# Retention and PReLU MLP on one core: scores and carried sums as one product of 128 rows, q and k turned by VectorE for all pairs from the second batch on

## The chip, the core and the metric

One core of a Trainium2 chip runs the whole program. The metric is the device time of one execution in microseconds (us). TensorE multiplies, VectorE, ScalarE and GpSimd (POOL) work elementwise, and SyncE (SP) issues nearly all transfers.

## What is computed

For 8 batches and 8 heads, q, k and v are 576 x 64 each. The attention is a retention with a decay of each head, without softmax; its output is one token-by-512 matrix, which goes through a two-layer MLP with a PReLU of 2048 features:

```python
scores = scale * np.matmul(q, k.transpose(0, 1, 3, 2))
gamma = 1.0 - 2.0 ** (-5.0 - np.arange(H, dtype=np.float32))
Dmat = np.where(rel >= 0, gamma[:, None, None] ** rel[None, :, :], 0.0)
attn_out = np.matmul(scores * Dmat[None, :, :, :], v)
x = attn_out.transpose(0, 2, 1, 3).reshape(B * S, H * D)     # 4608 x 512
h = x @ w_in
g = np.maximum(h, 0.0) + alpha * np.minimum(h, 0.0)
return g @ w_out
```

All data is fp32.

## The kernel before

**Attention.** A sequence is cut into NJ = 9 chunks of C = 64 positions, and two heads make a pair: 4 pairs for each batch, 32 in all. In a chunk the masked scores act on v directly; what earlier chunks bring comes through carried sums of k transposed times v (a 64 x 64 matrix for each chunk and head), which multiply q. The decay is put in by scaling q and v by powers of gamma, by a factor in the masked scores (L577) and in the running sums. The first batch (pairs 0 to 3) is worked in parts of its own (`part_...`, L627 to L772), which the change leaves as they are. Every other pair passes through these steps:

- *turning*: q and k have to stand with the 64 features on the partitions. For the pairs of batch 1 (4 to 7; `n < NEARLY`) they are loaded in natural order and TensorE turns them (`turn`, L542): five products with an identity (L552) for each of k and q, and two copies by ScalarE (L555). For the pairs from batch 2 on they are loaded in strips (`load_sq`, L84) of 32 features, so that VectorE's turn of 32 x 32 squares (L539) does it; k is then loaded a second time in natural order for the sums. GpSimd scales q (L534, or L515) and v (L515).
- `scores` (L564): 64 x 64 products for both heads, 20 for a pair (chunk 9 is done twice to fill the tile, L573), into two PSUM tiles, one for each head; VectorE scales and masks them into `at` (L577).
- `states` (L582): 16 products of 64 x 64 (L588), then ScalarE's copy (L593) and VectorE's running sums (L594, L597, L599) into `su`.
- `values` (L606): 18 products of v with the masked scores (L612), and on top of them in the same PSUM tiles 32 products of 64 rows and 32 columns with the sums as weights and q as the moving operand (L619). ScalarE puts the result into the token blocks `xb` (`put_x`, L503 and L505).

**MLP.** 18 blocks of 256 tokens. The first two are worked plainly (`plain_unit` L397, `plain_out` L376), while the weights arrive in 32 pieces that ScalarE, VectorE and GpSimd round (`piece_in`, `piece_out`). The other 16 use a product scheme with 7 products instead of 8 (`mlp_unit`): for each of 8 units of a block 14 products with 128 columns moving (L441), elementwise steps on ScalarE and VectorE (L447 to L463), and 7 products with 256 columns moving (L361), which are issued one unit later. At the end of a block VectorE combines the PSUM tiles (L347, L348), and two transfers store the block.

**What orders the work.** Up to L889 the order is the program's own. The 12 units of the plain stage (L874) have 21 gaps, and `gap` (L861) puts one step of the list `steps` into each: k, q, u (states), s, v for each of the four pairs of batch 1, with the scaling ahead of k. The loads of pair n + 2 are issued behind the values of pair n. From L894 on, the loop over pairs interleaves the attention of one batch with the MLP units of the blocks that are ready (`pop_units`): scores, units, states, units, the turning of the next pair, values, units; here a scheduler places the instructions. All PSUM tiles of the attention share one tag with two buffers (`ps_tile`, L520). `kT` and `at` have one buffer, `qT` and `su` two, and the loaded tiles two.

Of the kernel before, what the change touches and what calls it, by code (L numbers as in the profile page):

```python
# [18 lines left out]
def kernel(  # L19
# [49 lines left out]


    NEARLY = 2 * NPAIR

    def load_nat(t, src, b, c):
        hs, s0 = slice(2 * c, 2 * c + 2), (NM - 1) * P
        for h2 in range(2):
            nc.sync.dma_start(t[:, 0:NM - 1, h2],
                              src[b, 2 * c + h2, 0:s0].rearrange("(m p) d -> p m d", p=P))
        nc.sync.dma_start(t[0:C, NM - 1], src[b, hs, s0:S].rearrange("h p d -> p h d"))  # L80
# [9 lines left out]

    def load_pair(n):
        b, c = pairs[n]
        kn, vn, qx = [nat.tile([P, NM, 2, D], FP32, tag=f"nat_{x}", name=f"{x}n_{n}")
                      for x in "kvq"]
        if n < NEARLY:
            kx = kn
            load_nat(kn, k, b, c)
            load_nat(qx, q, b, c)
        else:
            kx = nat.tile([P, NB, 32], FP32, tag="sq_k", name=f"kx_{n}")  # L100
            qx = qx.rearrange("p m h d -> p (m h d)")[:, 0:S].rearrange(
                "p (n r) -> p n r", r=32)
            load_sq(kx, k, b, c)
            load_sq(qx, q, b, c)
            load_nat(kn, k, b, c)
        load_nat(vn, v, b, c)
        return kn, kx, qx, vn
# [55 lines left out]
    make_identity(nc, ident)  # L163

# [46 lines left out]
    tabx = const.tile([P, NPAIR, 2], FP32, name="tabx")  # L211
    for h2 in range(2):
        hd = slice(h2 * D, (h2 + 1) * D)
        nc.vector.tensor_copy(gch[hd, 0], th[hd, 2, h2:H:2])
        nc.vector.tensor_scalar(tabx[hd, :, 0], pf[hd, 0, h2:H:2], float(D) ** -0.5, None,
                                ALU.mult)
        nc.vector.scalar_tensor_tensor(out=tabx[hd, :, 1], in0=dif[hd, 5, h2:H:2], scalar=1.0,
                                       in1=tabx[hd, :, 0], op0=ALU.add, op1=ALU.mult)
# [272 lines left out]
    def put_x(b, c, par, pv):  # L491

        w = TB // C
        at = b * NJ
        m, nm = 0, NM - par
        while m < nm:
            kb, o = divmod(at + 2 * m + par, w)
            if kb not in xb:
                xb[kb] = ring.tile([P, NCC, TB], FP32, tag=f"x{kb % NRING}", name=f"xb_{kb}")
            n = min(nm - m, (w - o + 1) // 2)  # L500
            to = xb[kb][:, c].rearrange("p (j w) -> p j w", w=C)[:, o:o + 2 * n - 1:2]
            for h2 in range(2) if par else ():
                nc.scalar.copy(to[half(h2)], pv[half(1 - h2), m:m + n])  # L503
            if not par:
                nc.scalar.copy(to, pv[:, m:m + n])  # L505
            m += n
# [3 lines left out]


    def scale(t, x, c):
        for rows, m in ((P, slice(0, NM - 1)), (C, slice(NM - 1, NM))):
            n = m.stop - m.start
            nc.gpsimd.tensor_tensor(  # L515
                out=t[0:rows, m], in0=t[0:rows, m],
                in1=th[0:rows, x, None, 2 * c:2 * c + 2, None].to_broadcast([rows, n, 2, D]),
                op=ALU.mult)
# [4 lines left out]
    def scale_pair(n):  # L523
        c = pairs[n][1]
        scale(loaded[n][2], 0, c)
        scale(loaded[n][3], 1, c)

    def transposes(n):
        c = pairs[n][1]
        kn, kx, qx, vn = loaded[n]  # L530
        kT = attn.tile([P, S], FP32, tag="kT", name=f"kT_{n}")
        qT = attn.tile([P, S], FP32, tag="qT", bufs=2, name=f"qT_{n}")
# [4 lines left out]
        scale(vn, 1, c)  # L537
        for src, dst in ((kx, kT), (qx, qT)):
            nc.vector.transpose(dst, src.rearrange("p n r -> p (n r)"))  # L539
        return kT, qT  # L540

    def turn(n, i):  # L542

        src = loaded[n][i]
        dst = attn.tile([P, S], FP32, tag="qT" if i else "kT", bufs=2 if i else 1,
                        name=f"T{i}_{n}")
        for m0, m1 in ((0, 3), (3, NM)):
            w = min(m1 * P, S) - m0 * P
            pt = ps_tile([P, 3 * P], f"pt{i + m0}_{n}")
            for m in range(m0, m1):  # L550
                rows = min(P, S - m * P)
                nc.tensor.transpose(pt[:, (m - m0) * P:(m - m0) * P + rows],  # L552
                                    src[0:rows, m].rearrange("p h d -> p (h d)"),
                                    ident[0:rows, 0:rows])
            nc.scalar.copy(dst[:, m0 * P:m0 * P + w], pt[:, 0:w])  # L555
        return dst

    def half(x):
        return slice(x * C, (x + 1) * C)
# [4 lines left out]
    def scores(n, kT, qT):  # L564
        c = pairs[n][1]
        at = attn.tile([P, 2 * NM * C], FP32, tag="at", name=f"at_{n}").rearrange(
            "p (h m s) -> h p m s", h=2, s=C)
        ps = [ps_tile([P, NM, C], f"ps{h2}_{n}") for h2 in range(2)]
        for m in range(NM):
            for p2 in range(2):  # L570
                j = min(2 * m + p2, NJ - 1)
                for h2 in range(2):
                    nc.tensor.matmul(ps[h2][half(p2), m], kT[half(h2), chunk(j)],  # L573
                                     qT[half(h2), chunk(j)], start=True, stop=True)
        for h2 in range(2):
            h = 2 * c + h2
            nc.vector.scalar_tensor_tensor(  # L577
                out=at[h2], in0=ps[h2], scalar=th[:, 3, h:h + 1],
                in1=mask[:, None, :].to_broadcast([P, NM, C]), op0=ALU.mult, op1=ALU.mult)
        return at  # L580

    def states(n, kn, vn):  # L582
        c = pairs[n][1]
        ps = [ps_tile([P, NM - 1, D], f"pu{p2}_{n}") for p2 in range(2)]
        for m in range(NM - 1):
            for p2 in range(2):
                for h2 in range(2):
                    nc.tensor.matmul(ps[p2][half(h2), m], kn[half(p2), m, h2],  # L588
                                     vn[half(p2), m, h2], start=(m == 0), stop=(m == NM - 2),
                                     skip_group_check=True)  # L590
        su = attn.tile([P, NJ - 1, D], FP32, tag="su", bufs=2, name=f"su_{n}")
        g1, g2 = gch[:, 0, c:c + 1], gch[:, 1, c:c + 1]
        nc.scalar.copy(su[:, 0::2], ps[0])  # L593
        nc.vector.scalar_tensor_tensor(out=su[:, 1::2], in0=su[:, 0::2], scalar=g1, in1=ps[1],  # L594
                                       op0=ALU.mult, op1=ALU.add)
# [5 lines left out]
        return su  # L601

    def values(n, vn, qT, at, su):  # L606
        b, c = pairs[n]
        pv = [ps_tile([P, NM, C], f"pv{p2}_{n}") for p2 in range(2)]
        for m in range(NM):
            for p2 in range(2 if 2 * m + 1 < NJ else 1):  # L610
                for h2 in range(2):
                    nc.tensor.matmul(pv[p2][half(h2 ^ p2), m], vn[half(p2), m, h2],  # L612
                                     at[h2][half(p2), m], start=(m == 0), stop=False,
                                     skip_group_check=True)
        for j in range(1, NJ):
            for h2 in range(2):
                for e in range(0, D, 32):
                    to = (h2 ^ (j % 2)) * D + e
                    nc.tensor.matmul(pv[j % 2][to:to + 32, j // 2],  # L619
                                     su[half(h2), j - 1, e:e + 32], qT[half(h2), chunk(j)],  # L620
                                     start=False, stop=(j >= NJ - 2), skip_group_check=True)
        for p2 in range(2):
            put_x(b, c, p2, pv[p2])
# [215 lines left out]
    kq, ats, sus = {}, {}, {}  # L839

    def step(what, n):
        kn, _, _, vn = loaded[n]
        if what == "scale":
            scale_pair(n)
        elif what in "kq":
            kq[n] = kq.get(n, ()) + (turn(n, 0 if what == "k" else 2),)
        elif what == "s":
            ats[n] = scores(n, *kq[n])
        elif what == "u":
            sus[n] = states(n, kn, vn)  # L850
        elif what == "v":
            values(n, vn, kq[n][1], ats[n], sus[n])
            del loaded[n]
            if n + 2 <= NEARLY:
                loaded[n + 2] = load_pair(n + 2)

    steps = [(x, n) for n in range(NPAIR, NEARLY) for x in "kqusv"]
    scale_pair(NPAIR)
    scaled = [NPAIR + 1]

    def gap():  # L861

        for x, n in steps[0:3]:
            if x == "k" and n == scaled[0] and n in loaded:
                scaled[0] += 1
                step("scale", n)
        if steps:
            step(*steps.pop(0))
# [77 lines left out]
```

## Time and profile before

| | |
|---|---|
| median of 3 runs | 1047.41 us (1045.88 to 1048.51) |
| the profiled execution | 1043.84 us, its span 1042.1 us |
| granted TensorE clock | 0.997 |
| attention products of pairs 4 to 31, busy: values L612, L619 | 22.3 + 24.0 us |
| scores L573, states L588 | 22.7 + 19.4 us |
| turning on TensorE, L552 | 7.0 us |
| MLP products L441 and L361 | 491.2 and 407.8 us |
| squares on VectorE, L539 | 37.1 us for 48 |

Each row of the page's table of groups gives a line of the kernel, the engine and operation, the tiles, the shape and the number of instructions, then the busy time of the group, the mean time of one in ns, and the idle time of the engine just ahead of them with what ended it. Products overlap in the array: 1008 records of L612 with a mean of 223 ns are 22.3 us of busy time. So the cost of a block of small products is read from the timeline, from its first start to the start of what follows it. A product of fp32 operands leaves two records. PE is TensorE's row for products, PEld the one for loading weights.

### The profile page before, as it was taken

The numbers are of one execution on the slowest core, as the hardware profiler recorded it, in microseconds if no ns is written. First come the engines' busy times: TensorE is split into PE (matmuls) and PEld (weight loads), VectorE is DVE, ScalarE is ACT, GpSimd is POOL, SyncE is SP. The second block draws the span as 40 slices with busy tenths as digits, with TensorE's granted clock in tenths as the row PEclk, the third lists the DMA queues.
The fourth block names the chain that finished last, engine by engine and source line by source line (L and its number), as shares of the span: only waits on it lengthen the run. The fifth ranks groups of instructions, "written<-read, shape, count | busy, mean of one in ns | idle before, by whom it ended". The sixth has DMA issues, their size and how long they took to land.

```text
span 1042.1 us, 27067 instructions
## 1 busy us (share of the span) xinstructions
PE 1024.3 (98%) x11329; PEld 902.0 (87%) x11329; DVE 748.2 (72%) x1951; ACT 170.8 (16%) x533; POOL 214.8 (21%) x253
## 2 busy tenths in 40 slices
PE   5999999999999999999999999999999999999998
PEld 4766667999999999999999999999999999999997
DVE  7766755776786778776768777867777776766675
ACT  4545532111111110110110011111111111000000
POOL 4566675411301020200011111301030001010000
PEclk8999999999999999999999999999999999999999
DMA  9855605233232221121212232222222100000000
GB/s 244 252 153 139 163 20 122 41 68 64 48 67 45 59 47 44 35 56 24 56 36 50 42 68 46 57 47 53 62 40 52 24 22 2 21 1 22 1 21 21
DMA packets 216073, 63.36 MB, mean 61 GB/s; under 512 B 201088, under 2 KB 209296, under 8 KB 215952
## 3 DMA queue, kind: packets, MB, share of 16 engines
q1 hardware_dynamic: 213840, 61.11, 25.3%
q8 instruction: 89, 1.46, 0.6%
q10 hardware_dynamic: 2112, 0.53, 0.3%
q14 instruction: 32, 0.26, 0.1%
HBM read 52.17 MB, written 9.44 MB: 59 GB/s over the span
## 4 chain that ended last, share of the span: by engine, by line
PE 97%; DMA 1%; issue 1%; POOL 0%; DVE 0%; ACT 0%; SPq 0%; DVEq 0%; POOLq 0%
PE ph L441 40%; PE po L361 37%; PE ph L397 6%; PE po L376 5%; PE pv L619 2%; PE ps L573 2%; PE pv L612 2%; PE pu L588 2%; DMA w_out<-in_k_dram 1%; PE pt L552 0%; PE pt L653 0%; PE pv L726 0%; PE ps L672 0%; PE pv L715 0%; POOL w_out L304 0%
## 5 line engine op out<-in xcount | busy, mean ns | idle before, releaser
L361 PE MATMUL po<-w_out,g 128*128 128x256 f32 x1792 | 407.8, 379 | 0.0
L361 PEld LDWEIGHTS po<-w_out,g 128*128 128x128 f32 x1792 | 330.8, 190 | 39.7
L452 DVE TENSOR_TENSOR g<-ph,g 128x256 f32<-128x256 f32 (+1 forms) x512 | 187.4, 387 | 176.6 <-PE ph L441 95.7
L441 PE MATMUL ph<-xb,w_in 128*128 128x128 f32 x2048 | 277.6, 278 | 0.0
L441 PEld LDWEIGHTS ph<-xb,w_in 128*128 128x128 f32 x2048 | 253.2, 192 | 9.2 <-issue 0.7
L441 PE MATMUL ph<-xt,w_in 128*128 128x128 f32 x1536 | 213.6, 275 | 0.0
L441 PEld LDWEIGHTS ph<-xt,w_in 128*128 128x128 f32 x1536 | 192.2, 192 | 0.1
L463 DVE TENSOR_TENSOR g<-g 128x128 f32<-128x128 f32 x512 | 143.0, 320 | 7.8
L447 ACT COPY g<-ph 128x128 f32<-128x128 f32 x128 | 34.0, 265 | 462.2 <-PE ph L441 457.3
L515 POOL TENSOR_TENSOR vn<-vn,th 128x512 f32<-128x512 f32 (+1 forms) x56 | 39.7, 729 | 336.0 <-DMA vn<-in_v_dram 315.2
L455 DVE TENSOR_SCALAR g<-g,alpha 128x256 f32<-128x256 f32 x256 | 92.1, 402 | 4.5
L457 DVE SCALAR_TENSOR_TENSOR g<-g 128x512 f32<-128x512 f32 x128 | 91.8, 717 | 3.8
L397 PE MATMUL ph<-xb,w_in 128*128 128x256 f32 x256 | 61.1, 394 | 1.1 <-ACT xb L733 1.1
L427 POOL TENSOR_TENSOR xt<-xb,xt 128x256 f32<-128x256 f32 x32 | 25.2, 788 | 172.3 <-ACT xb L505 163.3
L376 PE MATMUL po<-w_out,g 128*128 128x512 f32 x128 | 59.0, 604 | 0.1
L397 PEld LDWEIGHTS ph<-xb,w_in 128*128 128x128 f32 x256 | 49.2, 196 | 10.0 <-issue 2.4
L503 ACT COPY xb<-pv 64x64 f32<-64x64 f32 (+1 forms) x144 | 33.9, 236 | 145.7 <-PE pv L619 143.9
L376 PEld LDWEIGHTS po<-w_out,g 128*128 128x128 f32 x128 | 23.1, 190 | 24.3 <-issue 22.5
L539 DVE STREAM_TRANSPOSE qT<-qn 128x576 f32<-128x576 f32 x24 | 18.7, 778 | 28.9 <-PE pv L619 23.1
L413 DVE SCALAR_TENSOR_TENSOR g<-g,nalpha,ph 128x256 f32<-128x256 f32 x32 | 13.9, 477 | 31.6 <-ACT ph L403 31.6
L534 POOL TENSOR_TENSOR qn<-qn,tabx 128x576 f32<-128x576 f32 x24 | 28.1, 1171 | 28.7 <-DMA qn<-in_q_dram 22.8
L427 POOL TENSOR_TENSOR xt<-xb 128x256 f32<-128x256 f32 x16 | 11.5, 722 | 107.3 <-PE ph L441 107.3
(127 smaller groups left out, 665.0 us busy)
## 6 DMA issues: line engine op xcount, KB each, us to landing
out_dram<-osb SPq DMA_DIRECT2D x36, 256.0 KB, 2.2
kn<-in_k_dram SPq DMA_DIRECT2D x56, 128.0 KB, 2.9
vn<-in_v_dram SPq DMA_DIRECT2D x56, 128.0 KB, 2.8
kx<-in_k_dram SPq DMA_DIRECT2D x96, 72.0 KB, 2.5
qn<-in_q_dram SPq DMA_DIRECT2D x96, 72.0 KB, 2.6
raw<-in_moe_w_in_dram SPq DMA_DIRECT2D x24, 256.0 KB, 4.2
raw<-in_moe_w_out_dram SPq DMA_DIRECT2D x10, 512.0 KB, 4.5
w_in<-in_moe_w_out_dram SPq DMA_DIRECT2D x6, 512.0 KB, 4.8
```

The costliest lines, as they stand in the source:

```text
L361: nc.tensor.matmul(acc[kb][n // 2][:, n % 2, :], g[:, x, :], w_out[i][:, y, :], start=(i == 0 and n % 2 == 0), stop=(i == NU - 1 and (n % ...
L376: nc.tensor.matmul(acc[kb][m], g[:, 2 * x + m], w_out[i][:, 2 * x:2 * x + 2].rearrange("p x f -> p (x f)"), start=(i == 0 and x == 0), sto ...
L397: nc.tensor.matmul(ph[:, x], w_in[i // UST][:, cc // 2 * 2 + x, i % UST, cc % 2], xb[kb][:, cc], start=(cc == 0 and x == 0), stop=(cc == N ...
L427: nc.gpsimd.tensor_tensor(out=o, in0=x0, in1=x1, op=ALU.subtract)
L441: nc.tensor.matmul(ph[m][:, o], w_in[i // UST][:, l, i % UST, cc], r[:, cc], start=(n in (0, 3) and cc == 0), stop=(n in (2, 6) and cc == ...
L447: nc.scalar.copy(g[:, 7], ph[0][:, 2])
L452: nc.vector.tensor_tensor(out=o, in0=x0, in1=x1, op=ALU.add)
L455: nc.vector.tensor_scalar(g[:, 4 + 2 * m:6 + 2 * m], g[:, 2 * m:2 * m + 2], 0.0, alpha[:, fc:fc + 1], ALU.min, ALU.mult)
L457: nc.vector.scalar_tensor_tensor(out=g[:, 0:4].rearrange("p x t -> p (x t)"), in0=g[:, 0:4].rearrange("p x t -> p (x t)"), scalar=0.0, in1 ...
L463: ins = nc.vector.tensor_tensor(out=g[:, o, :], in0=g[:, x0, :], in1=g[:, x1, :], op=op)
L503: nc.scalar.copy(to[half(h2)], pv[half(1 - h2), m:m + n])
L515: nc.gpsimd.tensor_tensor(out=t[0:rows, m], in0=t[0:rows, m], in1=th[0:rows, x, None, 2 * c:2 * c + 2, None].to_broadcast([rows, n, 2, D]) ...
```

## The change

All pairs from pair 4 on now take one path.

- Loading: every pair has q and k in strips (`kx`, `qx`), and k (`kn`) and v (`vn`) for each head with the chunk's 64 positions on the partitions; head 0 lies on the upper half of them, head 1 on the lower. 12 loads for a pair. In `vn` the other half of the partitions of each head is kept for the sums; its chunk 0 is filled with zeros by ScalarE.
- Scaling: GpSimd scales q alone, ScalarE scales v (`tabv`). This is a step of its own ("p"), before the values of the pair ahead.
- Scores: 18 products. Both heads of a chunk go to one PSUM tile, on different halves of its partitions, and the tiles alternate by chunk. ScalarE copies the turned q into one half of the partitions of `mt`; VectorE writes the masked scores into the other half, in four instructions.
- States: again 16 products; the first step of the sums is two instructions of 64 partitions. The sums take the buffer of `kT`, and ScalarE copies them into `vn` behind v.
- Values: one product of 128 rows (64 of v, 64 of the sums) and 64 columns for each chunk and head, 18 for a pair; ScalarE's copies into `xb` are three for a pair.
- Order: in the gaps of the plain stage the steps are t, s, u, p, v of each pair, with the turning "t" of the next pair right behind v. Pair 8 is turned there too, and one MLP unit now comes ahead of its scores.

```diff
-    NEARLY = 2 * NPAIR
+    def load_head(t, src, b, h):
+        nc.sync.dma_start(t, src[b, h].rearrange("(j t) d -> t j d", t=C))
+
     def load_pair(n):
         b, c = pairs[n]
...
+        load_sq(kx, k, b, c)
+        load_sq(qx, q, b, c)
+        for t, src in ((vn, v), (kn, k)):
+            for h2 in range(2):
+                load_head(t[half(1 - h2), h2] if t is vn else t[half(1 - h2)], src, b, 2 * c + h2)
+        for h2 in range(2):
+
+            nc.scalar.copy(vn[half(h2), h2, 0], zero[half(h2)])
...
     def scale_pair(n):
         c = pairs[n][1]
-        scale(loaded[n][2], 0, c)
-        scale(loaded[n][3], 1, c)
...
+        for h2 in range(2):
+            x = half(1 - h2)
+            nc.scalar.activation(vn[x, h2], vn[x, h2], ACTF.Copy, scale=tabv[x, c:c + 1])
...
-    def turn(n, i):
...
+    def pair_scores(n, kT, qT):
...
+        ps = [ps_tile([P, NM, C], f"ps{p2}_{n}") for p2 in range(2)]
+        for j in range(NJ):
+            for h2 in range(2):
+                x = (1 - h2, h2)[j % 2]
+                nc.tensor.matmul(ps[j % 2][half(x), j // 2], kT[half(h2), chunk(j)],
+                                 qT[half(h2), chunk(j)], start=True, stop=True)
         for h2 in range(2):
...
+            nc.scalar.copy(mt[half(h2), h2].rearrange("p j s -> p (j s)"), qT[half(h2)])
+        for p2 in range(2):
+            for h2 in range(2):
+                h, to, x = 2 * c + h2, half(1 - h2), (1 - h2, h2)[p2]
+                nm = NM - p2
+                nc.vector.scalar_tensor_tensor(
+                    out=mt[to, h2, p2::2], in0=ps[p2][half(x), 0:nm], scalar=th[to, 3, h:h + 1],
+                    in1=mask[to, None, :].to_broadcast([C, nm, C]), op0=ALU.mult, op1=ALU.mult)
+        return mt
...
-        su = attn.tile([P, NJ - 1, D], FP32, tag="su", bufs=2, name=f"su_{n}")
+        for j in range(NJ - 1):
+            for h2 in range(2):
+                x = (h2, 1 - h2)[j % 2]
+                nc.tensor.matmul(ps[j % 2][half(x), j // 2], kn[half(1 - h2), j],
+                                 vn[half(1 - h2), h2, j], start=True, stop=True)
+        su = attn.tile([P, S], FP32, tag="kT", name=f"su_{n}")[:, 0:S - D].rearrange(
+            "p (j d) -> p j d", d=D)
...
+        for h2 in range(2):
+            nc.scalar.copy(vn[half(h2), h2, 1:], su[half(h2)])
+
+    def pair_values(n, vn, mt):
         b, c = pairs[n]
...
-        for j in range(1, NJ):
+        for j in range(NJ):
             for h2 in range(2):
-                for e in range(0, D, 32):
-                    to = (h2 ^ (j % 2)) * D + e
-                    nc.tensor.matmul(pv[j % 2][to:to + 32, j // 2],
-                                     su[half(h2), j - 1, e:e + 32], qT[half(h2), chunk(j)],
-                                     start=False, stop=(j >= NJ - 2), skip_group_check=True)
...
+                nc.tensor.matmul(pv[j >= j1][half(h2), j - (j1 if j >= j1 else 0)],
+                                 vn[:, h2, j], mt[:, h2, j], start=True, stop=True)
...
-    steps = [(x, n) for n in range(NPAIR, NEARLY) for x in "kqusv"]
...
+    last = 2 * NPAIR - 1
+    steps = [(("t", NPAIR),)]
+    for n in range(NPAIR, last + 1):
+        steps += [(("s", n),), (("u", n),), (("p", n + 1),), (("v", n), ("t", n + 1)), ()]
...
+        if n == last + 1:
+            pop_units(1)
...
         if n + 1 < len(pairs):
+            scale_pair(n + 1)
             turned[n + 1] = transposes(n + 1)
-        values(n, vn, qT, at, su)
+        pair_values(n, vn, mt)
```

## The prediction, made before the changed kernel ran

> **What bounds the kernel now.** I read the page's busy shares first, then its chain of waits, then TensorE's own waits, and last the timeline of TensorE around one pair.
>
> ```profile
> PE 1024.3 (98%) x11329; PEld 902.0 (87%) x11329; DVE 748.2 (72%) x1951; ACT 170.8 (16%) x533; POOL 214.8 (21%) x253
> ```
> ```profile
> PE 97%; DMA 1%; issue 1%; POOL 0%; DVE 0%; ACT 0%; SPq 0%; DVEq 0%; POOLq 0%
> ```
> ```profile
> PE pt L653 <- DMA w_out<-in_k_dram: 6.1, 2, 5.0
> ...
> PE ps L573 <- DVE qT L539: 2.3, 1, 2.3
> ```
>
> TensorE is busy 98% and owns 97% of the chain. Behind the start (the 6.1 us for the first k) it waits once for over 1.2 us: 2.3 us in front of the scores of pair 8, for the transposed q. So what an attention block costs is the time it keeps TensorE's stream of MLP products away. In the timelines (start, duration, line, number of records; one matrix product leaves two records):
>
> ```profile
> 700.86 3.19 PE L361 MATMUL po<-w_out,g 128*128 128x256 f32 x14
> 703.98 0.69 PE L588 MATMUL pu<-vn,kn 64*64 64x64 f32 x32
> 704.60 1.16 PE L441 MATMUL ph<-xb,w_in 128*128 128x128 f32 x8
> ...
> 707.83 3.19 PE L361 MATMUL po<-w_out,g 128*128 128x256 f32 x14
> 710.95 0.80 PE L612 MATMUL pv<-at,vn 64*64 64x64 f32 x36
> 711.68 0.86 PE L619 MATMUL pv<-qT,su 64*32 64x64 f32 x64
> 712.46 1.16 PE L441 MATMUL ph<-xb,w_in 128*128 128x128 f32 x8
> ...
> 715.69 3.19 PE L361 MATMUL po<-w_out,g 128*128 128x256 f32 x14
> 718.81 0.81 PE L573 MATMUL ps<-qT,kT 64*64 64x64 f32 x40
> 719.55 1.16 PE L441 MATMUL ph<-xb,w_in 128*128 128x128 f32 x8
> ```
> ```profile
> 53.56 0.68 PE L761 MATMUL pv<-w_out,w_out 64*64 64x64 f32 x16
> 54.17 0.65 PE L768 MATMUL pv<-w_out,w_out 64*32 64x64 f32 x32
> 54.75 0.70 PE L376 MATMUL po<-w_out,g 128*128 128x512 f32 x1
> ```
> ```profile
> 68.63 0.80 PE L552 MATMUL pt<-ident,kn 128*128 128x128 f32 x5
> 69.36 3.70 PE L376 MATMUL po<-w_out,g 128*128 128x512 f32 x8
> 72.90 3.62 PE L397 MATMUL ph<-xb,w_in 128*128 128x256 f32 x16
> ```
>
> Read starts against the next starts. States (L588, 32 records) hold the stream 704.60 - 703.98 = 0.62 us, scores (L573, 40 records) 0.74, values 712.46 - 710.95 = 1.51. Eight records more cost 0.12 us: the four 64x64 quadrants of the array run at once, four records in a round of about 0.058 us, so 0.62 is 8 rounds and 0.74 is 10, with a constant of some 0.15 in each. L761 settles the price of two column halves: its outputs lie in two column halves and all its rows in one row half, so two tiles are in use, and its 16 records take 0.61 us, as long as the 32 of L588: 8 rounds of two. Besides, each block pays about 0.09 us before its first record and 0.1 us in the first product behind it, and so will the new ones.
>
> **The change, part by part**, on TensorE first.
>
> Values. Removed: 18 products of L612 and 32 of L619, 1.51 us with the switch between their two shapes. Added: 18 products of 128 rows and 64 columns, alternating between the column halves, 36 records. The trace of before has no such shape. The nearest row is L761: two column halves over the same rows, two at a time. By it 36 records are 18 rounds, 0.62 + 10 x 0.058 = 1.20 us, a gain of 0.31 to 0.32. The bad end: one record at a time, 36 rounds, 0.62 + 28 x 0.058 = 2.24 us, a loss of 0.73. The good end: going in and out of tiles with all 128 rows could be cheaper by the 0.09 + 0.1, a gain of 0.5. I take L761's: 28 pairs x 0.32 = 9.0 us.
>
> Scores. 18 products for 20, the last two without partners: 8 full rounds and 2 half ones, 10 as before. A start or two is saved (0.01 us a pair, 0.4 us in all). States: 16 products, 8 rounds, nothing.
>
> A rule speaks against these two. In the Trainium skill, "TensorEngine Tiling (Array Packing)", Restrictions and Gotchas, Gotcha 1, different row tiles cannot access the same PSUM bank at the same time. Before, L573 and L588 gave each row half its own bank; now both row halves of a chunk write one bank, in different column halves. If the rule held here, only two records could run at once: 8 rounds more in each block, 16 x 0.058 = 0.93 us a pair, 26 us in all. But L768 does the same in this trace: its two row halves write one bank, in different columns, and its 32 records take 54.75 - 54.17 = 0.58 us, 8 rounds of four; two at a time would be about 1.08. I go by the row: nothing lost.
>
> Turning q and k of the four pairs of batch 1. Eight blocks of five products (L552) go: 69.36 - 68.63 = 0.73 us each. The eight L376 records behind take 72.90 - 69.36 = 3.54, against 3.43 where no block precedes (61.91 to 65.34 in the chain), so 0.1 more goes with it: 8 x 0.84 = 6.7 us. TensorE has no idle time in 78 to 156 us but for the blocks, so this comes off the path.
>
> The wait of 2.3 us. Pair 8 was turned only when its own turn came, behind the subtractions on GpSimd (q scaled 163.45 to 164.55, turned from 164.62). Now its q is scaled one gap ahead of the values of pair 7, it is turned right behind those values, and its scores come one whole unit later (L441 and L376, over 6 us). Gain 2.3; nothing would be late next, since the operand xt of that unit keeps its place. If GpSimd were late all the same, this gain alone would go.
>
> Sum on TensorE: 9.0 + 0.4 + 6.7 + 2.3 = 18.4 us.
>
> Beside TensorE. VectorE: the masked scores become four instructions of 256 to 320 elements (0.48 and 0.54 us by L594 and L577) for two: 2.0 us for 1.1. The first step of the sums is cut in two: +0.48. Together 1.4 us a pair of some 27 us; the four early pairs also get two squares (0.77 each, L539). VectorE is busy 42.0 of 56 us in 600 to 656 and 13 to 19 of 26 in 78 to 156, so it stays under about 85%. ScalarE gets per pair: zeros (2 x 0.21), v scaled (2 x 0.64), q copied into the joint operand (2 x 0.64), the sums copied behind v (2 x 0.58), 4.1 us, and saves 0.9 of L503/L505 and, early, 1.6 of L555. It is busy 7.0 of 56, early 13 of 26. GpSimd loses the scaling of v (1.04 + 0.42) and early that of q. SyncE issues 12 loads a pair, each about 0.5 (L87: 2.06 for 4), for 14 late and 9 early: 6 us of issue either way. In the early stage more and smaller packets come in (DMA share 0.50 to 0.65); the pieces are fetched six ahead, so I cost that at nothing; uncovered, it would be a wait of a microsecond or two.
>
> The new waits. ScalarE's copy of the sums waits for VectorE's chain, with the g copy (L447) of a later unit queued behind it, for which VectorE waits. Worked on the shown pair: states end 704.5, sums copied 705.13, two first steps to 706.1, three of 0.33 and L452 (0.42) to 707.6, the last step 708.0, two copies to 709.2. The values start at 710.95 - 0.03, 1.7 us later, so the copy is covered by the unit between. If VectorE also has the 2.9 us of an output block (seven of L347/L348 at 0.42) in that unit, the values stay covered, since those are queued behind the sums, but g comes close to when L361 needs it. In the built order ScalarE's part of the output block falls between the sums and the values in few pairs. Bounds: nothing, and 14 output blocks x 0.5 us = 7. By the slack of the pair shown I take 0.5 us in all. k's turned tile now shares its buffer with the sums, so VectorE's square of the next k waits for those two copies, with the rest of that unit's g behind it: about 0.2 us, against 2.5 us until L361 takes g.
>
> So -17.9 us. The profiled execution took 1043.84 us (span 1042.1), which gives 1025.9; the median of the runs is 1047.41, 3.6 above it, and gives **1029.5 us**.
>
> **The rivals.**
> (a) The joint product runs one tile at a time. Place: the values block; price: +0.73 instead of -0.32 in 28 pairs. That is -17.9 + 9.0 + 20.4 = +11.5, **1059 us**, slower than before. It decides from about 29 rounds on (8.9 us of other gains over 28 pairs is 0.32 us, so 1.51 + 0.32 = 1.83 us, 29 rounds). For it: all 128 rows with 64 columns occur nowhere in this trace. Against it: L761 shares its rows and is not serial, and in the quadrant blocks each row half also carries two streams.
> (b) The bank rule holds: -17.9 + 26 = +8, **1055 us**. Against it: L768.
> (c) The chain states, sums, copy, values or the fuller queues of ScalarE and VectorE hold TensorE up now and then: 0.1 to 0.4 us at each of 28 pairs, 3 to 11 us, **1033 to 1040 us**. For it: slack falls from 4 us to 1.7. Against it: ScalarE is at 16%.
> (d) The early stage is paced by its weight pieces, so the turns give nothing: -11.2, **1036 us**. Against it: no wait of L376 or L397 for a piece in TensorE's list.
>
> **How the numbers follow.** My forecast 0.77 (1024 to 1033: the cheaper switch at one end, a few waits at the other), (c) and (d) 0.13 together, (a) 0.05, (b) 0.04, some other fault 0.01. The range 1024 to 1041 takes in the forecast, (c) and (d). A measurement here can tell about 0.3%, 3.1 us, from no change. Faster 0.88: forecast, most of (c) and (d); same 0.02; slower 0.10: (a), (b) and the rest.
>
> **What would show it.** In the profile after: the values block from its first start to the next L441 start at 1.2 us (2.2 says (a)); states 0.62 and scores 0.73 (over 1.0 says (b)); no transposes on TensorE behind 70 us; no wait in front of the scores of pair 8; no wait of the values for ScalarE's copy in TensorE's list (some of 0.1 us or more says (c)). I would be wrong above all if the 128-row tiles need a switch or a rate that no row here shows.

## The result, and the profile after

The changed kernel takes 1030.34 us (median of 4 runs, 1028.04 to 1031.11) beside 1046.91 for the kernel before in the same set. The ratio is 0.9837, with a 95% interval of 0.9816 to 0.9857: 16.6 us saved by the medians, 15.0 to 19.3 by the interval (1046.91 x 0.0143 to 0.0184). Forecast were 17.9 us saved, which lies inside the interval, and 1029.5. A second set on another occasion gave 1030.46 (ratio 0.9852). The profiled execution took 1030.42 us.

TensorE is still what ends the kernel. The page's busy line, its chain by engine, and then TensorE's waits:

```profile
PE 1008.3 (98%) x9385; PEld 890.2 (87%) x9385; DVE 771.7 (75%) x2045; ACT 267.2 (26%) x597; POOL 173.4 (17%) x194
```
```profile
PE 92%; DVE 2%; issue 1%; DMA 1%; ACT 1%; SPq 1%; POOL 0%; ACTq 0%; DVEq 0%; POOLq 0%
```
```profile
PE pv L688 <- issue: 4.4, 2, 3.2
PE ph L395 <- ACT vn L100: 1.2, 1, 1.2
...
PE po L374 <- DVE g L411: 0.8, 1, 0.8
PE ph L395 <- issue: 0.8, 1, 0.8
PE pu L547 <- DVE mt L536: 0.4, 1, 0.4
```

1944 records fewer, but only 16 us less busy time: most of what is gone ran beside something. The wait for the q of pair 8 is gone. Two waits are new and belong to the change: 1.2 us in front of a unit of the plain stage (L395), put down to ScalarE, and 0.4 us in front of a block of states (L547), put down to VectorE's reading of the scores. Around them the chain runs through the other engines, and TensorE's share of it is 92% for 97% before. The waits of L688, of L374 for L411 and for "issue" (nothing that the profile shows) lie in the first 45 us, in code that the change leaves alone. The one of L688 is not new: in the kernel before it is L726, with 2.9 us the longest wait behind the start, which the prediction's list passes over.

The timeline of TensorE around the same kind of pair as before: states, values, scores.

```profile
692.23 0.69 PE L547 MATMUL pu<-vn,kn 64*64 64x64 f32 x32
692.85 1.16 PE L439 MATMUL ph<-xb,w_in 128*128 128x128 f32 x8
...
699.20 1.27 PE L574 MATMUL pv<-mt,vn 128*64 128x64 f32 x36
700.39 1.16 PE L439 MATMUL ph<-xb,w_in 128*128 128x128 f32 x8
...
706.74 0.80 PE L528 MATMUL ps<-qT,kT 64*64 64x64 f32 x36
707.47 1.16 PE L439 MATMUL ph<-xb,w_in 128*128 128x128 f32 x8
```

From start to next start: states 0.62 as before, values 1.19 for 1.51, scores 0.73 for 0.74. All 28 pairs show the same three numbers within 0.01 us, but for the one block of states with its wait, which takes 1.30.

**Where the time went, by stage.** The first 60 us of the kernel differ from one execution to the next by more than the effects sought: the first unit of the plain stage that has gaps starts between 57.4 and 63.2 us in the ten profiles of this study, and at 59.5 and 63.2 in the two profiles of one and the same kernel (e6_defer and e4_defer below). Part of it is the granted clock: its mean from 10 to 55 us is 0.96 in the profile that gets there first (e2_banks), 0.92 in those of the kernel before and the changed one, and 0.89 in the one that gets there last (e4_defer). So I cut each profile at that start and at the first start of a unit of the later scheme (L441, L439), and compare the stretches. For the kernel before and then the changed one (start and end of the stretch, its length, then busy us of each engine with its number of instructions, the granted clock, the busy share of the DMA engines and what they moved):

```profile
core 0: us, PE busy (x) PEld busy (x) DVE busy (x) ACT busy (x) POOL busy (x), PEclk, DMA share, GB/s
58.29:161.52 103.23, 103.23 (x1018) 68.50 (x1016) 61.50 (x110) 49.25 (x119) 68.64 (x74) 1.00 0.43 113
161.52:1042.10 880.58, 874.05 (x9513) 798.45 (x9511) 641.82 (x1735) 92.38 (x363) 119.05 (x147) 1.00 0.20 43
```
```profile
60.45:157.78 97.33, 95.78 (x706) 63.23 (x705) 76.02 (x131) 58.62 (x113) 64.01 (x63) 1.00 0.58 139
157.78:1028.70 870.92, 866.04 (x7881) 792.50 (x7879) 651.31 (x1806) 178.22 (x429) 82.30 (x98) 1.00 0.19 42
```

The plain stage is 5.9 us shorter, with VectorE now busy 78% of it instead of 60%. Behind it, up to the start of the last product, 875.97 us became 865.66: 10.3 less. The start cost 2.2 us more in this execution, and the end (last product to the end of the span) 0.6.

### The profile page after: what moved, and what is told of

Read it like the earlier page. It is cut to its first block, busy times and chain, and to the rows that moved or that the text cites. A ratio compares the mean times of both kernels' runs of the same rounds, so it can differ in the third digit from the quotient of the medians.

```text
span 1028.7 us, 23097 instructions
## 1 busy us (share of the span) xinstructions
PE 1008.3 (98%) x9385; PEld 890.2 (87%) x9385; DVE 771.7 (75%) x2045; ACT 267.2 (26%) x597; POOL 173.4 (17%) x194
## 4 chain that ended last, share of the span: by engine, by line
PE 92%; DVE 2%; issue 1%; DMA 1%; ACT 1%; SPq 1%; POOL 0%; ACTq 0%; DVEq 0%; POOLq 0%
PE ph L439 40%; PE po L359 38%; PE ph L395 3%; PE po L374 3%; PE pv L574 3%; PE ps L528 2%; PE pu L547 2%; DMA w_out<-in_q_dram 1%; DMA w_in<-in_moe_w_out_dram 0%; SPq L77 0%; DVE wc L288 0%; DVE mt L536 0%; DVE wc L285 0%; PE pv L688 0%; ACT wa L274 0%
## 5 line engine op out<-in xcount | busy, mean ns | idle before, releaser
L439 PE MATMUL ph<-xb,w_in 128*128 128x128 f32 x2048 | 277.7, 279 | 0.0
L439 PEld LDWEIGHTS ph<-xb,w_in 128*128 128x128 f32 x2048 | 253.1, 192 | 8.2 <-issue 0.5
L439 PE MATMUL ph<-xt,w_in 128*128 128x128 f32 x1536 | 213.3, 275 | 0.0
L439 PEld LDWEIGHTS ph<-xt,w_in 128*128 128x128 f32 x1536 | 192.1, 192 | 0.0
L461 DVE TENSOR_TENSOR g<-g 128x128 f32<-128x128 f32 x512 | 127.6, 290 | 7.8
L453 DVE TENSOR_SCALAR g<-g,alpha 128x256 f32<-128x256 f32 x256 | 84.9, 374 | 3.7
L500 POOL TENSOR_TENSOR qx<-qx,tabx 128x576 f32<-128x576 f32 x28 | 32.9, 1174 | 310.0 <-DMA qx<-in_q_dram 274.5
L395 PE MATMUL ph<-xb,w_in 128*128 128x256 f32 x256 | 60.3, 389 | 3.1 <-ACT vn L100 1.2
L536 DVE SCALAR_TENSOR_TENSOR mt<-ps,th,mask 64x320 f32<-64x320 f32 (+1 forms) x112 | 57.8, 516 | 4.5 <-PE ps L528 2.7
L395 PEld LDWEIGHTS ph<-xb,w_in 128*128 128x128 f32 x256 | 48.8, 194 | 13.3 <-issue 3.4
L374 PE MATMUL po<-w_out,g 128*128 128x512 f32 x128 | 58.5, 600 | 0.8 <-DVE g L411 0.8
L505 ACT ACTIVATE vn<-vn,tabv 64x576 f32<-64x576 f32 x56 | 43.3, 773 | 15.2 <-DMA vn<-in_v_dram 14.1
L563 ACT COPY vn<-su 64x512 f32<-64x512 f32 x56 | 34.5, 616 | 48.5 <-DVE su L560 47.9
L374 PEld LDWEIGHTS po<-w_out,g 128*128 128x128 f32 x128 | 23.5, 190 | 24.9 <-issue 22.5
L583 ACT COPY xb<-pv 128x256 f32<-128x256 f32 (+3 forms) x84 | 22.7, 321 | 78.9 <-PE pv L574 78.8
```

The costliest lines, as they stand in the source:

```text
L374: nc.tensor.matmul(acc[kb][m], g[:, 2 * x + m], w_out[i][:, 2 * x:2 * x + 2].rearrange("p x f -> p (x f)"), start=(i == 0 and x == 0), sto ...
L395: nc.tensor.matmul(ph[:, x], w_in[i // UST][:, cc // 2 * 2 + x, i % UST, cc % 2], xb[kb][:, cc], start=(cc == 0 and x == 0), stop=(cc == N ...
L439: nc.tensor.matmul(ph[m][:, o], w_in[i // UST][:, l, i % UST, cc], r[:, cc], start=(n in (0, 3) and cc == 0), stop=(n in (2, 6) and cc == ...
L453: nc.vector.tensor_scalar(g[:, 4 + 2 * m:6 + 2 * m], g[:, 2 * m:2 * m + 2], 0.0, alpha[:, fc:fc + 1], ALU.min, ALU.mult)
L461: ins = nc.vector.tensor_tensor(out=g[:, o, :], in0=g[:, x0, :], in1=g[:, x1, :], op=op)
L505: nc.scalar.activation(vn[x, h2], vn[x, h2], ACTF.Copy, scale=tabv[x, c:c + 1])
```

## The experiments

The kernel before ran beside each of them, and every ratio is to that kernel.

**e1_heads: one head after the other.** Which tiles neighbours in the stream use, with the same products:

```diff
-        for j in range(NJ):
-            for h2 in range(2):
+        for h2 in range(2):
+            for j in range(NJ):
                 nc.tensor.matmul(pv[j >= j1][half(h2), j - (j1 if j >= j1 else 0)],
```

> The changed kernel with the 18 joint products of a pair in another order: all of one head, then all of the other, so that neighbours in the stream use the same column half. Same products, same output. Theory: the block of values is cheap because neighbours in different column halves run side by side and TensorE starts products in order; then this order leaves one tile busy at a time, 36 rounds instead of 18, about 2.24 us a block instead of 1.20, and the run is about 29 us slower than the changed kernel, near 1059 us. Rival: each tile has its own queue and takes its products whatever their order in the stream; then the block stays near 1.2 us and the time near 1030.

Measured: 1052.72 us, ratio 1.0051 (1.0036 to 1.0066): slower than the kernel before. Its timeline of TensorE:

```profile
714.35 2.13 PE L574 MATMUL pv<-mt,vn 128*64 128x64 f32 x36
716.42 1.16 PE L439 MATMUL ph<-xb,w_in 128*128 128x128 f32 x8
```

The block takes 2.06 us instead of 1.19, and the stretch behind the plain stage 886.4 us instead of 865.7: 24 pairs x 0.86 = 20.7. The four pairs of the plain stage add 1.7 us for 3.4, since no wait of TensorE is left there. So nearly the whole block runs one product at a time, and the gain of the change rests on the order of the two loops. That supports the theory over the rival; but the run is 22 us slower than the changed kernel, not 29, and 2.06 is 33 rounds, not the 36 that I expected. In the trace three rounds around the change of head run in twos, and a record as long as the first of a block (270 ns for 222) starts three records ahead of the second head's place in the stream, so products seem to be taken a few places ahead.

**e2_banks: a bank for each row half.**

```diff
-                nc.tensor.matmul(ps[j % 2][half(x), j // 2], kT[half(h2), chunk(j)],
+                nc.tensor.matmul(ps[h2][half(x), j // 2], kT[half(h2), chunk(j)],
...
-                    out=mt[to, h2, p2::2], in0=ps[p2][half(x), 0:nm], scalar=th[to, 3, h:h + 1],
+                    out=mt[to, h2, p2::2], in0=ps[h2][half(x), 0:nm], scalar=th[to, 3, h:h + 1],
```

> The changed kernel with the scores written as before by row half: each of the two row halves has its own PSUM bank, instead of both sharing the bank of a chunk; VectorE reads the other bank accordingly. States keep their shared banks. Theory (the rule on banks does not hold for different column halves): the block of scores stays at 0.73 us from its first start to the next, time unchanged, 1030 us within 2. Rival (the shared bank costs something): the block gets shorter, by up to 0.1 us, 3 us in all.

Measured: 1030.91 us (0.9831 to 0.9871 of before). TensorE's timeline:

```profile
703.72 0.80 PE L528 MATMUL ps<-qT,kT 64*64 64x64 f32 x36
704.45 1.16 PE L439 MATMUL ph<-xb,w_in 128*128 128x128 f32 x8
```

0.73 us, the same as in the changed kernel. Here two row halves write one bank at once, in different column halves, and lose nothing by it; the rule that the prediction weighed does not hold for these products, and the measurement decides.

**e3_turns: eight blocks of transposes back.** Constants are turned in the gaps of the plain stage and read by nobody.

```diff
+    def idle_turn(n):
+        for x in range(2):
+            pt = ps_tile([P, 3 * P], f"dt{x}_{n}")
+            for m in range(3 - x):
+                nc.tensor.transpose(pt[:, m * P:(m + 1) * P], ident, ident)
...
-        steps += [(("s", n),), (("u", n),), (("p", n + 1),), (("v", n), ("t", n + 1)), ()]
+        steps += [(("s", n),), (("u", n),), (("p", n + 1), ("d", n)), (("v", n), ("t", n + 1)),
+                  (("d", n + 100),)]
```

> The changed kernel with eight blocks of five 128x128 transposes of a constant put back into the gaps of the plain stage, where nobody reads them; two a pair. VectorE's squares stay. Theory (the stage is paced by TensorE, and turning there cost 0.73 + 0.1 us a block): 6.7 us slower than the changed kernel, near 1037. Rival (the stage is now partly paced by waits for ScalarE and VectorE, which the blocks would fill): 4 us or less.

Measured: 1036.31 us, 6.0 above the 1030.34 of the changed kernel and 5.4 above e2_banks of the same set (ratio 0.9896, 0.9881 to 0.9911). Its plain stage is 102.4 us, 5.1 longer. From TensorE's waits:

```profile
PE dt L807 <- DVE su L560: 2.0, 3, 0.9
```

The blocks themselves wait 2.0 us for the PSUM tiles that VectorE's sums still read, and the 1.2 us in front of L395 and the 0.4 in front of the states are gone from the list: the added work covers waits that were there. The size lies between theory (6.7) and rival (4 or less), and what the rival names, waits that the blocks fill, is what the trace shows.

**e5_turnonly: the kernel before with the turning changed.** Loads in strips and VectorE's squares for pairs 4 to 7; the order k, q, u, s, v stays, with t for k and nothing for q. The edit does one thing more than its expectation says: it takes out the step that had GpSimd scale q and v ahead of k, so that they are scaled in step t itself, right in front of the squares.

```diff
-        if n < NEARLY:
+        if False:
...
-        elif what in "kq":
-            kq[n] = kq.get(n, ()) + (turn(n, 0 if what == "k" else 2),)
+        elif what == "t":
+            kq[n] = transposes(n)
...
-    steps = [(x, n) for n in range(NPAIR, NEARLY) for x in "kqusv"]
-    scale_pair(NPAIR)
-    scaled = [NPAIR + 1]
+    steps = [(x, n) for n in range(NPAIR, NEARLY) for x in "t-usv"]
...
-        for x, n in steps[0:3]:
-            if x == "k" and n == scaled[0] and n in loaded:
-                scaled[0] += 1
-                step("scale", n)
```

> The kernel before with one part of the change alone: the four pairs of batch 1 are loaded in strips and turned by VectorE, like the later ones; separate products for scores and sums, scaling and the late turning of pair 8 as before. Theory (turning on TensorE cost 0.84 us in each of eight blocks): 6.7 us below the kernel before, about 1040, with the wait of 2.3 us for the q of pair 8 still there. Rival (most of the gain of the change in the plain stage was that wait and the joint product): 3 us or less.

Measured: 1046.54 us, ratio 0.9999 (0.9987 to 1.0012): nothing at all. My expectation failed; the rival's 3 us or less came, but not for its reason, as the next run shows. The plain stage is 102.55 us for 103.23. TensorE lost its eight blocks (6.7 us) and got 4.7 us of waits in their place, 4.0 of them inside the four blocks of scores, which besides hold TensorE 0.3 us longer each, since each stops behind its first product. (Behind the plain stage this profile takes 1.7 us more than the kernel before; its granted clock is 0.74 from 167.5 to 174 us, where it is 1.00 in the other.) One block of scores in the timeline, the total in the list of waits, and what VectorE does ahead of that block:

```profile
85.18 0.32 PE L573 MATMUL ps<-qT,kT 64*64 64x64 f32 x2
86.52 0.81 PE L573 MATMUL ps<-qT,kT 64*64 64x64 f32 x38 [1.02 <-DVE su L599]
87.26 1.13 PE L376 MATMUL po<-w_out,g 128*128 128x512 f32 x2
```
```profile
PE ps L573 <- DVE su L599: 3.0, 3, 1.4
```
```profile
75.49 0.78 DVE L539 STREAM_TRANSPOSE qT<-qn 128x576 f32<-128x576 f32 x1 [2.12 <-POOL qn L534]
...
83.83 2.21 DVE L597 SCALAR_TENSOR_TENSOR su<-su,gch 128x64 f32<-128x64 f32 x3
```

Scores take their two PSUM tiles one gap behind the states. The states' tiles are freed by VectorE's last sum (L599), whose chain in this order stands behind the rounding of weight pieces. Without the turning blocks TensorE comes to the scores earlier, and VectorE doesn't. Two things make VectorE later still. In three of the four turns it stands for GpSimd's scaling of q, 5.6 us in all. And the three short steps of the sums (L597) take 2.1 to 3.0 us in each of the four pairs, for 0.93 in the late pair of the kernel before, while GpSimd works beside them (see the last section); in the block shown that excess alone is more than the wait. No run takes away one of the two alone.

**e7_order: the same, in the order of the changed kernel.** Separate products still; scores ahead of the states, values two gaps behind them, scaling in a step of its own one gap ahead, pair 8 turned behind the values of pair 7. Against e5_turnonly, in extracts:

```diff
-        if what == "scale":
-            scale_pair(n)
+        if what == "p":
+            scale_sq(n)
...
-    steps = [(x, n) for n in range(NPAIR, NEARLY) for x in "t-usv"]
+    steps = [(("t", NPAIR),)]
+    for n in range(NPAIR, NEARLY):
+        steps += [(("s", n),), (("u", n),), (("p", n + 1),), (("v", n), ("t", n + 1)), ()]
...
+        if n == NEARLY:
+            pop_units(1)
```

> The kernel of e5_turnonly (separate products, batch 1 turned by VectorE) with the order of the plain stage that the changed kernel has: scores ahead of the states, the values two gaps behind the states, scaling one gap ahead, the turning right behind the values of the pair ahead, and pair 8 turned there with one unit ahead of its scores. Theory (without the turning products TensorE runs into VectorE's sums, since the scores, one gap behind the states, need the PSUM tile that the sums still read; the other order removes that wait, and the 2.3 us of pair 8): 7 to 9 us below the kernel before, near 1038. Rival (VectorE's load with four squares more, whatever the order, paces the stage): 0 to 3 us below it.

Measured: 1036.81 us, ratio 0.9909 (0.9894 to 0.9923): 9.6 us below the kernel before. The plain stage is 96.6 us:

```profile
59.91:156.50 96.59, 96.59 (x977) 64.13 (x976) 70.72 (x119) 44.38 (x103) 70.14 (x73) 1.00 0.53 130
```

The stretch behind it, to the start of the last product, is 873.6, 2.4 less than before, which is the wait of pair 8; the two stretches together give 9.0. No wait of the scores is left in TensorE's list. VectorE's busy time is 70.7 us here and 70.6 in e5_turnonly, so its load did not pace the stage; where the steps stand did. The turning on VectorE is worth its 6.6 us only together with the new places of the steps, the scaling among them: which of these counts for how much is not shown. The new order without VectorE's turning was not run; in the plain stage of the kernel before TensorE has no wait that it could have saved.

**e4_defer, e6_defer: the copies of the sums one gap later.** In the changed kernel the wait of 1.2 us begins here, in ScalarE's timeline (the last numbers are its idle time before the instruction); the two rows behind it are VectorE's last reading of the unit's PSUM tile, and the unit of TensorE that waits:

```profile
103.61 0.38 ACT L552 COPY su<-pu 128x256 f32<-128x256 f32 x1
108.97 1.26 ACT L563 COPY vn<-su 64x512 f32<-64x512 f32 x2 [4.97 <-DVE su L560]
110.25 0.69 ACT L274 ACTIVATE wa<-raw 128x512 f32<-128x512 f32 x1
...
112.65 1.56 ACT L505 ACTIVATE vn<-vn,tabv 64x576 f32<-64x576 f32 x2
114.12 0.57 ACT L399 ACTIVATE g<-ph 128x512 f32<-128x512 f32 x1
```
```profile
115.29 0.86 DVE L411 SCALAR_TENSOR_TENSOR g<-g,nalpha,ph 128x256 f32<-128x256 f32 x2
```
```profile
116.30 3.69 PE L395 MATMUL ph<-xb,w_in 128*128 128x256 f32 x16 [1.19 <-ACT vn L100]
```

ScalarE stands 5.0 us at the copy of the sums, then rounds two weight pieces and scales v, and comes to the relus of a unit (L399) at 114.12, 3.9 us after the unit's products ended at about 110.2. VectorE's step behind the relus (L411) ends at 116.15. The next unit (L395) needs that PSUM tile, of which there is one, and waits from 115.1 to 116.3. The trace names ScalarE's L100 as what ended the wait, since it ended last (116.25); but L100 writes zeros into a `vn` that the unit does not read, so by the program it is L411. The edit takes the two copies out of step u of the plain stage and puts them into the next gap:

```diff
-        for h2 in range(2):
-            nc.scalar.copy(vn[half(h2), h2, 1:], su[half(h2)])
+        if put:
+            put_sums(su, vn)
+        return su
...
-        steps += [(("s", n),), (("u", n),), (("p", n + 1),), (("v", n), ("t", n + 1)), ()]
+        steps += [(("s", n),), (("u", n),), (("c", n), ("p", n + 1)), (("v", n), ("t", n + 1)), ()]
```

For e4_defer:

> The changed kernel with ScalarE's two copies of the sums into v put off by one gap in the plain stage alone, so that ScalarE does not stand at them while VectorE makes the sums, with the rounding of two weight pieces and the two relus of a unit queued behind. Theory: the wait of 1.2 us of a unit for its PSUM tile (in front of L395 at 116 us) and the 5 us idle time of ScalarE at that copy go; 1 to 1.5 us faster than the changed kernel, near 1029. Rival (the queue of VectorE, not ScalarE's wait, is what makes the relus late): the wait stays, at the same or another place, and the time is the same.

For e6_defer, the same kernel in a later set:

> The kernel of e4_defer once more, beside the changed kernel on the same chip: the two copies of the sums one gap later in the plain stage. Theory: 1 to 2 us below the changed kernel, by the waits of 1.2 and 0.4 us that it loses. Rival: the 3 us of e4_defer were the spread of the first 60 us, and the two are equal.

For a2_after, the changed kernel in that set:

> The changed kernel once more, unedited, beside the other runs of this set, for a comparison on one chip. 1030 us within 2 (16 to 18 us below the kernel before). The stretch up to the first unit of the plain stage with gaps (58 to 63 us in the profiles so far, in code that the change leaves alone) is expected to differ by some us between executions, and the stage behind it to take the same.

Measured: 1027.27 and, in a second set, 1027.25 us (ratios 0.9817, 0.9794 to 0.9840, and 0.9825, 0.9807 to 0.9844), beside 1030.46 for the changed kernel in that set (0.9852, 0.9834 to 0.9870). The intervals overlap, but the profiles agree: the plain stage is 95.2 us in both runs of this kernel and 97.3 in both of the changed one, and in its list of waits only those of the first 47 us are left.

```profile
59.52:154.73 95.21, 95.21 (x705) 63.21 (x704) 75.53 (x131) 58.19 (x113) 64.10 (x63) 1.00 0.61 141
```

TensorE is busy in all of the stage, and in e6_defer it owns 97% of the chain again. 2.1 of the 3 us are shown in this way; the rest is within the spread. It is the fastest version of this study.

## Why the prediction was right

- *Values, 9.0 us.* Right in size and in reason: 1.19 us came for 1.20. The other end, one product at a time, was priced at 2.24; e1_heads shows it at 2.06. Rival (a) was a real danger: the shape can run so, and only the order of two loops keeps it from that. It would have made the kernel slower than before, as e1_heads is.
- *Scores and states, 0.4 us.* Right (0.73 and 0.62). Rival (b), the bank rule, fell with these two numbers, and e2_banks shows that separate banks gain nothing.
- *The wait of pair 8, 2.3 us.* Right: 873.6 for 876.0 in e7_order. With it, 24 pairs x 0.335 = 8.0 us make 10.3, and the stretch behind the plain stage is 10.3 us shorter.
- *Turning of batch 1, 6.7 us.* Right in size, with a reason that was too short. "TensorE has no idle time in 78 to 156 us" says who paces the stage, not how near the next one is. In e5_turnonly nearly the whole gain went into waits, most of them for VectorE. That the change keeps it is owed to the other places of the steps, the scaling among them, which I took for a detail; so far as the prediction goes, that was luck.
- *New waits, 0.5 us.* Here the sum was mis-sized: the plain stage gave back 2.1 us, the two waits and what they add to the products behind them. It should have become shorter by 6.7 and by 4 x 0.335 = 1.3, 8.0 in all; 5.9 came, and with the copies put off 8.0. The mechanism stood in rival (c) ("ScalarE's copy of the sums waits for VectorE's chain"). I had worked its slack on a late pair, where it holds (no such wait in 24 pairs), and carried the answer to the stage where VectorE also rounds weight pieces. "The pieces are fetched six ahead, so I cost that at nothing" did hold: TensorE waits for no piece, with the DMA share of the stage at 0.58 for 0.43.

The sum of these is 8.0 - 2.1 + 10.3 = 16.2 us, without the start and the end of the kernel; the medians differ by 16.6. So the forecast of 17.9 did not come near by two errors that cancel: the gains were summed to 18.4 and are 18.3, and the one term that was off is that of the new waits. Rival (d), that the weight pieces pace the stage, fell with e7_order.

## What to carry to other kernels

Cost a block of small products by rounds over the tiles in use, from a row of the same kind, and then look at the order in the stream: neighbours have to be in different tiles. When work is taken off the bound engine, ask in that very stage how far the next engine is behind, and which buffer it still holds; here the same 6.6 us came or didn't by where five steps and a scaling stood. A copy put behind a chain of another engine also holds up what is queued behind it, so it belongs where its input is already there.

## What the hardware showed unexpectedly

The 64-element steps of the sums (L558, two operands in SBUF) are not always short. In the changed kernel's profile they take 0.28 us as a rule and up to 1.3:

```profile
L558 DVE SCALAR_TENSOR_TENSOR su<-su,gch x84: 272/284/1314, 85.1 to 861.7; 128x64 f32<-128x64 f32 x84
```

The 72 that run while GpSimd is idle have a mean of 0.28 us, the 12 that overlap with a GpSimd instruction 0.68. In the kernel before it is 77 of 0.28 and 7 of 0.78, in e5_turnonly 72 of 0.28 and 12 of 0.95. In front of the wait of L395 above three of them take 2.57 us, with GpSimd's combination of weights (L302, 1.3 us each) at the same time. The Trainium skill says in "SBUF — State Buffer", Who interferes with whom, that VectorE and GpSimd take turns on a shared pair of ports, one of them standing still for a whole instruction of the other; under "SBUF: two separate sides" it counts VectorE's operations with two SBUF inputs among those, against a GpSimd instruction that reads SBUF. The numbers fit that, but no run here took GpSimd's work away, so it is not shown apart.
